# Random-feature attention ahead of a gated MLP: q, k and v loaded in runs of 512 bytes

## The chip, the core and the metric

The kernel runs on one core of a Trainium2 chip. A core has five instruction engines, each of which works through its own queue in order and waits on semaphores for the others: TensorE (PE; matmuls and transposes, with the loading of weights listed apart as PEld), VectorE (DVE), ScalarE (ACT), GpSimd (POOL) and SyncE (SP), which here issues all DMAs. Matmuls write to PSUM, all other data lies in SBUF, and 16 DMA engines move data between SBUF and device memory. The metric is the device time of one execution in microseconds; before and after are compared by the median of several runs. A profiled execution gives the trace: start, length and releaser of every instruction, and the clock that TensorE was granted.

## What is computed

The reference, cut to its core (m is 128 random features, D is 64, eight batches, eight heads, 576 positions):

```python
scale = 1.0 / np.sqrt(np.sqrt(D))
def phi(x):
    proj = np.einsum('bhsd,md->bhsm', x, omega)
    h = proj - np.sum(x * x, axis=-1, keepdims=True) / 2.0
    h = h - np.max(h, axis=-1, keepdims=True)
    return np.exp(h) / np.sqrt(m)
q_p, k_p = phi(q * scale), phi(k * scale)
kv = np.einsum('bhsm,bhsd->bhmd', k_p, v)
z = np.sum(k_p, axis=2)
num = np.einsum('bhsm,bhmd->bhsd', q_p, kv)
den = np.einsum('bhsm,bhm->bhs', q_p, z)[..., None] + 1e-06
x = num / den    # then 4608 rows of 512, heads side by side
g = x @ w_gate
out = (g * (1.0 / (1.0 + np.exp(-g))) * (x @ w_val)) @ w_out
```

The weights are stored as 64-bit floats (512 x 1536, 512 x 1536 and 1536 x 512); q, k, v and omega as 32-bit.

## The kernel before

**Attention.** Work goes in groups of G = 256 positions of a pair of heads (512 values of 64: four blocks of 128 rows, CH = 2 chunks for each of two heads). 576 is 2 x 256 + 64, so a batch has eight such groups and one group of rests (`gr is None`) with the last 64 positions of all eight heads. A step takes two groups at once: in the first six steps two of k, then one of q and one of k, at the end two of q. There are 72 steps. Step n goes through these functions, some of them a step or more late (KLAG, NLAG and the like):

- `load` (into `nat`) and `load_v` (into `v0` to `v7`, or `vrest`), both by `load_group`. Position r + 2p + c stands on partition p as chunk c: two neighbouring positions of a head are 512 contiguous bytes in memory. Before, the tile's layout is (chunk, head, 64), so that each of them is a run of 256 bytes of its own.
- `st_transpose`: four transposes (L370) turn a `nat` into `pt`, ACT copies it to `x` (L378), POOL squares `nat` into `sq` (L377).
- `st_project`: 16 matmuls with omega into `pp` (L393), one for each group, chunk and half of the 128 partitions. A half of the partitions is one of the two heads.
- `st_max`: DVE sums the squares (L404), takes the maxima (two of L411 a step) and makes the bias `st` (L413, L414). `st_exp`: ACT takes eight exponentials (L425) into the features `ph`.
- `k_accumulate`: matmuls of `ph` with a block of `v` (L528) into the PSUM tile `kvacc`, which holds four heads. A block of v has 65 columns, the last being ones, so that column 64 collects z. When all of a batch's positions are in, `kv_finalize` lets ACT copy the tile to `kvr` (L441), 16 times in all. In batches 4 to 7 PE then transposes z out of it (`zp`, L447), and z goes by way of device memory to a tile `zt` on all partitions.
- q's side: `q_transpose` (`ptq`, L552, copied to `qt`). In batches 0 to 3 `q_mult` multiplies by the 65 columns of `kvr` and divides by the last one; in batches 4 to 7 `q_den` multiplies `ph` by `zt` on POOL (`jk`, L488), DVE sums it, and `q_norm` scales `ph`. `q_out` writes the result as `x` of the MLP, split in two parts `xh` and `xl` whose sum it is.

**Weights.** They come as pairs of 32-bit words. `convert_all` loads each of 36 pieces raw (tile `st0` to `st11`, a name shared with the statistics; L225 for w_gate), makes 32-bit floats of it in one step on ACT (`wc`, L260), five on DVE (L262 to L270) and one on POOL (L272), and stores it. Later the pieces are read back and split into `whi` and `wlo` (L242, L243).

**MLP.** `stream` goes over tiles of 256 or 512 rows and sets of three 128-column blocks of the hidden width: three products for each of gate (`g`, L641) and value (`v`, L641; the same letter as the attention's v in a trace's rows), then `hh` and `hl` (L724, L725), then the product with w_out (`o`, L650).

**Order.** A table of steps says how much of the MLP and how many ticks of the conversion stand between the parts of a step (`CLOSE` for the first steps, `GROUPED` after). The order in which the rows of the program reach each engine's queue is not this one alone: the tile framework moves instructions by a cost model of its own, in which the length of a load counts. So an edit to a load can move instructions of other engines.

Of the kernel before, what the change touches and what calls it, by code (L numbers as in the profile page):

```python
# [23 lines left out]
def kernel(  # L24
# [76 lines left out]

    NR = S // G
    kgroups = [(pr, t * G) for pr in range(NPAIR) for t in range(NR)]
    kgroups.insert(len(kgroups) // 2, None)
# [18 lines left out]

    def pairs_of(gr):
        return [(2 * c, 2 * c + 1) for c in range(CH)] if gr is None else [gr[:1]] * CH

# [177 lines left out]

    vtile = [att.tile([P, CH, 2, VW], F32, name=f"v{i}", bufs=1) for i in range(NVF)]
    vrest = [att.tile([P, 2 * CH, 2, VW], F32, name=f"vrest{i}", bufs=1) for i in range(1)]
    for t in vtile:
        nc.gpsimd.memset(t[:, :, :, D:VW], 1.0)
    for t in vrest:
        nc.gpsimd.memset(t, 0.0)
        for c in range(CH):
# [7 lines left out]
    def load_group(t, src, b, gr, v_):  # L325
        if gr is not None:
            pr, r = gr
            nc.sync.dma_start(
                t[:, :, :, 0:D],
                src[b, 2 * pr : 2 * pr + 2, r : r + G, :].rearrange("h (p c) d -> p c h d", c=CH),  # L330
            )
            return
        for c in range(CH):
            for j, pr in enumerate(pairs_of(gr)[c]):
                nc.sync.dma_start(
                    t[j * RES : (j + 1) * RES, 2 * c + j if v_ else c, :, 0:D],
                    src[b, 2 * pr : 2 * pr + 2, S - RES : S, :].rearrange("h p d -> p h d"),
                )
# [98 lines left out]

    def kv_finalize(b, a2):
        acc = kvacc.pop((b, a2))
        raw = att.tile([P, 4, VW], F32, name=f"kvr{b}_{a2}", tag="kvr", bufs=4)  # L440
        nc.scalar.copy(raw, acc)  # L441
        for j in range(2):
            kvst[b, 2 * a2 + j] = raw[:, 2 * j : 2 * j + 2, :]
        if b >= BPOOL:

            zp = ps_att(f"zp{b}_{a2}", [4, P])
            nc.tensor.transpose(zp, raw[:, :, D], ident)  # L447
            zs = att.tile([4, P], F32, name=f"zs{b}_{a2}", tag="zs")
            nc.scalar.copy(zs, zp)
            zd = dram.tile([4, P], F32, name=f"zd{b}_{a2}", tag="zd", bufs=4)  # L450
            nc.sync.dma_start(zd, zs)
            zds[b, a2] = zd
# [18 lines left out]
    def q_den(n):  # L471

        n -= JLAG
        for _, b, g, gr in slots(n, "q"):
            if b < BPOOL:
                continue
            ph = box["q", b, g].rearrange("p c (h m) -> p c h m", m=M)
            jk = att.tile([P, CH, 2, M], F32, name=f"jk{b}_{g}", tag="jx")
            if gr is None:
                for c in range(CH):  # L480
                    for j, pr in enumerate(pairs_of(gr)[c]):
                        rows = slice(j * RES, (j + 1) * RES)
                        zt = zbc[b, pr // 2][rows, 2 * (pr % 2) : 2 * (pr % 2) + 2, :]
                        nc.gpsimd.tensor_tensor(jk[rows, c], ph[rows, c], zt, op=ALU.mult)
            else:
                pr = gr[0]
                zt = zbc[b, pr // 2][:, 2 * (pr % 2) : 2 * (pr % 2) + 2, :]
                nc.gpsimd.tensor_tensor(  # L488
                    jk, ph, zt.rearrange("p (o h) m -> p o h m", o=1).broadcast_to([P, CH, 2, M]), op=ALU.mult
                )  # L490
            dn = att.tile([P, 3, CH, 2], F32, name=f"dj{b}_{g}", tag="dj", bufs=6)
            nc.vector.tensor_reduce(dn[:, 0], jk, axis=AX.X, op=ALU.add)
            nc.vector.tensor_scalar_add(dn[:, 1], dn[:, 0], EPS)
            nc.vector.reciprocal(dn[:, 2], dn[:, 1])
            dns[b, g] = dn
# [14 lines left out]
    def k_accumulate(n, half):  # L510
# [3 lines left out]
        for b, g, gr, c in ks[half * len(ks) // 2 : (half + 1) * len(ks) // 2]:  # L514
# [4 lines left out]
            for j, pr in enumerate(pairs_of(gr)[c]):  # L519
                a2 = pr // 2  # L520
                first = (b, a2) not in kvacc
                if first:
                    kvacc[b, a2] = ps_k.tile([P, 4, VW], F32, name=f"kvacc{b}_{a2}", tag="kv")
                acc = kvacc[b, a2]
                done.setdefault((b, a2), []).append(pr)
                last = LAST[pr] == (g, c)
                for hh in range(2):
                    nc.tensor.matmul(  # L528
                        acc[:, 2 * (pr % 2) + hh, :],
                        ph[:, c, hh * M : (hh + 1) * M],  # L530
                        vt[:, 2 * c + j if gr is None else c, hh, :],
                        start=first and hh == 0,
                        stop=last,
                        skip_group_check=True,
                    )
# [6 lines left out]

    def q_transpose(n):
        m = n
        todo = [(b, g) for _, b, g, gr in slots(n - TLAG, "q") if b < BPOOL]
        todo += [(b, g) for _, b, g, gr in slots(n - NLAG, "q") if b >= BPOOL]
        for b, g in todo:
            ph = box.pop(("q", b, g))
            pt = (ps_moe if m < EARLY else ps_att)(f"ptq{b}_{g}", [P, 2, G])
            for hh in range(2):  # L550
                for c in range(CH):
                    nc.tensor.transpose(pt[:, hh, c * P : (c + 1) * P], ph[:, c, hh * M : (hh + 1) * M], ident)  # L552
            qts[b, g] = att.tile([P, 2, G], F32, name=f"qt{b}_{g}", tag="qt")
            nc.scalar.copy(qts[b, g], pt)

# [291 lines left out]
```

## Time and profile before

| | us |
|---|---|
| three runs | 1250.28, 1251.25, 1261.83 |
| median | 1251.25 |
| profiled execution | 1254.07 |
| its span, first to last instruction | 1252.3 |
| DVE, ACT, POOL: share of the span busy | 42%, 48%, 40% |
| DMA: packets; of them under 512 B | 157,692; 119,680 |
| DMA: moved, mean rate | 97.80 MB, 78 GB/s |

The page gives busy time for each engine, then slices of the span in tenths, and the chain of work that ended last. Rows of groups name line, engine, operation, output <- input and count. In rows of waits the first name waits for the second, then total time, times and the longest. Rows of the timeline give start, length, engine and line, with the idle time ahead in brackets. "SPq" is SP's issuing of a DMA. TensorE's granted clock is 1.00 at full speed and 0.50 at half.

### The profile page before, as it was taken

What the parts mean: (1) busy time and instruction counts of PE and PEld (TensorE: products, weight loads), DVE (VectorE), ACT (ScalarE), POOL (GpSimd) and SP (SyncE); (2) the same over time, 40 slices, a digit from 0 to 9 for tenths busy, and PEclk for the clock granted to TensorE, in tenths of its full rate; (3) what the DMA queues carried; (4) which work ended last, traced back from release to release, by engine and by line L of the source; (5) the groups of instructions that cost most, each with busy time, mean ns of one, the idle gap of its engine ahead of it and who ended that gap; (6) DMA issues with size and microseconds to landing.
All of it is one profiled execution on the core that took longest, in us unless ns stands there. A gap on an engine that the chain in (4) does not pass through costs nothing.

```text
span 1252.3 us, 19047 instructions
## 1 busy us (share of the span) xinstructions
PE 1217.5 (97%) x7137; PEld 1013.1 (81%) x7137; DVE 530.8 (42%) x1080; ACT 599.4 (48%) x1344; POOL 506.3 (40%) x448
## 2 busy tenths in 40 slices
PE   6999999999999999999999998999999999999998
PEld 5988877888778888778788876888787778888887
DVE  4887696556752344334434342233433311111112
ACT  3787755554354554556555443564644323221211
POOL 3333443645362213445544432554654314242421
PEclk7999999999999999999999998999999999999999
DMA  6555555343442222222222321221211111010112
GB/s 162 146 122 157 149 135 176 105 141 115 127 126 64 53 71 64 66 66 63 73 52 60 82 52 31 69 59 52 58 43 34 36 24 51 26 51 26 51 31 54
DMA packets 157692, 97.80 MB, mean 78 GB/s; under 512 B 119680, under 2 KB 132000, under 8 KB 157600
## 3 DMA queue, kind: packets, MB, share of 16 engines
q1 hardware_dynamic: 157600, 96.59, 29.0%
q8 instruction: 56, 0.92, 0.3%
q14 instruction: 36, 0.29, 0.1%
HBM read 77.66 MB, written 18.89 MB: 77 GB/s over the span
## 4 chain that ended last, share of the span: by engine, by line
PE 68%; DVE 2%; POOL 1%; ACT 1%; issue 0%; DMA 0%; SPq 0%; POOLq 0%; DVEq 0%
PE o L650 19%; PE g L641 19%; PE v L641 19%; PE pp L393 3%; PE kvacc L528 2%; PE ptq L552 2%; PE xt L607 2%; PE pt L370 1%; PE po L569 1%; POOL hl L725 1%; DVE st L266 0%; DMA nat<-in_k_dram 0%; DVE sl L721 0%; ACT ph L425 0%; DVE st L411 0%
## 5 line engine op out<-in xcount | busy, mean ns | idle before, releaser
L725 POOL TENSOR_TENSOR hl<-sl,hh 128x512 fp32r<-128x512 f32 (+1 forms) x120 | 142.3, 1190 | 208.0 <-ACT hh L724 207.9
L641 PE MATMUL g<-xh,whi 128*128 128x512 f32 (+1 forms) x480 | 181.6, 379 | 1.7 <-DVE sl L721 1.7
L641 PE MATMUL v<-xh,whi 128*128 128x512 f32 (+1 forms) x480 | 180.1, 375 | 2.7 <-DVE acc L674 2.7
L641 PE MATMUL g<-xh,wlo 128*128 128x512 f32 (+1 forms) x480 | 178.1, 372 | 0.0
L641 PE MATMUL g<-xl,whi 128*128 128x512 f32 (+1 forms) x480 | 178.1, 371 | 0.0
L243 POOL TENSOR_TENSOR wlo<-wraw,whi 128x512 fp32r<-128x512 f32 x108 | 139.0, 1299 | 95.6 <-ACT whi L242 94.1
L641 PE MATMUL v<-xh,wlo 128*128 128x512 f32 (+1 forms) x480 | 177.4, 370 | 0.0
L641 PE MATMUL v<-xl,whi 128*128 128x512 f32 (+1 forms) x480 | 177.3, 369 | 0.0
L650 PE MATMUL o<-whi,hh 128*128 128x512 f32 x432 | 173.4, 401 | 2.8 <-ACT hh L724 2.8
L425 ACT ACTIVATE ph<-pp,st 128x128 f32<-128x128 f32 x576 | 157.9, 384 | 32.8 <-DVE st L414 32.5
L650 PE MATMUL o<-whi,hl 128*128 128x512 f32 x432 | 170.6, 395 | 2.4 <-POOL hl L725 2.4
L650 PE MATMUL o<-wlo,hh 128*128 128x512 f32 x432 | 169.8, 393 | 0.0
L724 ACT CAST hh<-sl 128x512 fp32r<-128x512 f32 (+1 forms) x120 | 69.5, 581 | 207.5 <-DVE sl L721 207.1
L721 DVE TENSOR_TENSOR sl<-v,sl 128x512 f32<-128x512 f32 (+1 forms) x120 | 75.7, 633 | 181.3 <-PE v L641 179.3
L674 DVE TENSOR_TENSOR acc<-o,acc 128x512 f32<-128x512 f32 x108 | 74.1, 689 | 185.1 <-PE o L650 185.0
L377 POOL TENSOR_TENSOR sq<-nat 128x512 f32<-128x512 f32 x72 | 77.8, 1081 | 179.2 <-DMA nat<-in_k_dram 132.0
L411 DVE TENSOR_REDUCE st<-pp 128x4 f32<-128x512 f32 x144 | 93.7, 683 | 51.2 <-PE pp L393 51.0
L242 ACT CAST whi<-wraw 128x512 fp32r<-128x512 f32 x108 | 66.4, 623 | 100.0 <-PE v L641 61.2
L641 PEld LDWEIGHTS v<-xh,whi 128*128 128x128 f32 x480 | 90.6, 189 | 20.1 <-DVE acc L674 3.1
L641 PEld LDWEIGHTS g<-xh,whi 128*128 128x128 f32 x480 | 90.9, 190 | 19.7 <-issue 2.7
L641 PEld LDWEIGHTS g<-xh,wlo 128*128 128x128 f32 x480 | 91.0, 190 | 16.0 <-issue 0.4
L641 PEld LDWEIGHTS v<-xh,wlo 128*128 128x128 f32 x480 | 90.5, 189 | 15.2
(67 smaller groups left out, 1886.0 us busy)
## 6 DMA issues: line engine op xcount, KB each, us to landing
wraw<-wscr SPq DMA_DIRECT2D x108, 256.0 KB, 2.7
wscr<-wc SPq DMA_DIRECT2D x36, 256.0 KB, 2.3
out_dram<-acc SPq DMA_DIRECT2D x72, 128.0 KB, 2.3
nat<-in_k_dram SPq DMA_DIRECT2D x64, 128.0 KB, 3.0
v<-in_v_dram SPq DMA_DIRECT2D x64, 128.0 KB, 3.0
nat<-in_q_dram SPq DMA_DIRECT2D x64, 128.0 KB, 2.7
st<-in_moe_w_gate_dram SPq DMA_DIRECT2D x12, 512.0 KB, 5.2
st<-in_moe_w_val_dram SPq DMA_DIRECT2D x12, 512.0 KB, 4.2
```

What stands on the lines that cost most here:

```text
L242: nc.scalar.copy(hi, raw)
L243: nc.gpsimd.tensor_tensor(lo, raw, hi.bitcast(F32), op=ALU.subtract)
L377: nc.gpsimd.tensor_tensor(sq, nat, nat, op=ALU.mult)
L393: nc.tensor.matmul(pp[hh][:, i, c, :], x[r, i, c * P : (c + 1) * P], omT[r], start=True, stop=True)
L411: nc.vector.tensor_reduce(st[:, 1, :, :, hh], pp[hh], axis=AX.X, op=ALU.max, negate=True)
L425: nc.scalar.activation(ph[:, c, hh * M : (hh + 1) * M], pp[hh][:, i, c, :], AF.Exp, bias=st[:, 3, i, c, hh : hh + 1], scale=1.0,)
L641: nc.tensor.matmul(ps, a_[:, ws], b_[:, c, :], start=n == 0, stop=n == 3 * NC - 1)
L650: nc.tensor.matmul(ps, a_[:, ts_], b_, start=first and n == 0, stop=last and n == 2)
L674: nc.vector.tensor_tensor(a_, po, a_, op=ALU.add)
L721: nc.vector.tensor_tensor(h, pv, h, op=ALU.mult)
L724: nc.scalar.copy(hh, h)
L725: nc.gpsimd.tensor_tensor(hl, h, hh.bitcast(F32), op=ALU.subtract)
```

## The change

Chunks lie inside heads. The layout of a loaded group becomes (head, chunk, 64), so that two neighbouring positions of a head land as one run of 512 bytes. The transposes (L370) take the same addresses as before, but what comes out has the two positions on the two halves of the partitions and the two heads as blocks, so a projection's half is now a chunk. A small function `place` tells the readers of `ph` where chunk c of head hh stands.

v's tile becomes (head, 130): one column of ones, two chunks of 64, one column of ones. The block of chunk 0 is columns 0 to 64 with the ones ahead, that of chunk 1 is columns 65 to 129 with the ones behind. So the accumulator gets 66 columns: chunk 0 writes columns 0 to 64, chunk 1 columns 1 to 65, and z arrives in two parts. `kv_finalize` copies 4 x 66 columns and adds column 0 to column 65 on POOL. The group of rests stays as it was.

```diff
+    def place(gr, c, hh):
+        return (c, hh) if gr is None else (hh, c)
...
-    vtile = [att.tile([P, CH, 2, VW], F32, name=f"v{i}", bufs=1) for i in range(NVF)]
+    vtile = [att.tile([P, 2, 1 + CH * D + 1], F32, name=f"v{i}", bufs=1) for i in range(NVF)]
...
-        nc.gpsimd.memset(t[:, :, :, D:VW], 1.0)
+        for o in (0, 1 + CH * D):
+            nc.gpsimd.memset(t[:, :, o : o + 1], 1.0)
...
-                t[:, :, :, 0:D],
-                src[b, 2 * pr : 2 * pr + 2, r : r + G, :].rearrange("h (p c) d -> p c h d", c=CH),
+                t[:, :, 1 : 1 + CH * D] if v_ else t.rearrange("p h c d -> p h (c d)"),
+                src[b, 2 * pr : 2 * pr + 2, r : r + G, :].rearrange("h (p c) d -> p h (c d)", c=CH),
...
-        raw = att.tile([P, 4, VW], F32, name=f"kvr{b}_{a2}", tag="kvr", bufs=4)
-        nc.scalar.copy(raw, acc)
+        both = att.tile([P, 4, 1 + VW], F32, name=f"kvr{b}_{a2}", tag="kvr", bufs=4)
+        nc.scalar.copy(both, acc)
+        raw = both[:, :, 1:]
+        nc.gpsimd.tensor_tensor(raw[:, :, D], raw[:, :, D], both[:, :, 0], op=ALU.add)
...
-                    jk, ph, zt.rearrange("p (o h) m -> p o h m", o=1).broadcast_to([P, CH, 2, M]), op=ALU.mult
+                    jk, ph, zt.rearrange("p h (o m) -> p h o m", o=1).broadcast_to([P, 2, CH, M]), op=ALU.mult
...
-                    kvacc[b, a2] = ps_k.tile([P, 4, VW], F32, name=f"kvacc{b}_{a2}", tag="kv")
+                    kvacc[b, a2] = ps_k.tile([P, 4, 1 + VW], F32, name=f"kvacc{b}_{a2}", tag="kv")
...
+                    e, o = place(gr, c, hh)
+
+                    z = 0 if gr is not None and c == 0 else 1
                     nc.tensor.matmul(
-                        acc[:, 2 * (pr % 2) + hh, :],
-                        ph[:, c, hh * M : (hh + 1) * M],
-                        vt[:, 2 * c + j if gr is None else c, hh, :],
+                        acc[:, 2 * (pr % 2) + hh, z : z + VW],
+                        ph[:, e, o * M : (o + 1) * M],
+                        vt[:, 2 * c + j, hh, :] if gr is None else vt[:, hh, c * VW : (c + 1) * VW],
...
-                    nc.tensor.transpose(pt[:, hh, c * P : (c + 1) * P], ph[:, c, hh * M : (hh + 1) * M], ident)
+                    e, o = place(gr, c, hh)
+                    nc.tensor.transpose(pt[:, hh, c * P : (c + 1) * P], ph[:, e, o * M : (o + 1) * M], ident)
```

The order of instructions moves in the first part of the program. The lines of the changed program are numbered 6 to 14 higher there: L404, L411, L413 and L414 are L412, L419, L421 and L422, and L260 to L272 are L266 to L278.

DVE's queue near its start, before. `st_0` and `st_1` are statistics of steps 0 and 1, `pp0` and `pp1` the two halves of a projection, `wc0_0` the first weight piece in conversion and `st0_0` its raw words:

```order
L404 TENSOR_REDUCE st_2_221<-sq_2_222 128x8
L411 TENSOR_REDUCE st_0_142<-pp0_0_151 128x4
L411 TENSOR_REDUCE st_0_142<-pp1_0_152 128x4
L404 TENSOR_REDUCE st_3_263<-sq_3_264 128x8
L413 SCALAR_TENSOR_TENSOR st_0_142<-st_0_142 128x8
L411 TENSOR_REDUCE st_1_176<-pp0_1_203 128x4
L414 SCALAR_TENSOR_TENSOR st_0_142<-st_0_142 128x8
L411 TENSOR_REDUCE st_1_176<-pp1_1_204 128x4
L413 SCALAR_TENSOR_TENSOR st_1_176<-st_1_176 128x8
L262 TENSOR_SCALAR wc0_0_167<-wc0_0_167 128x512
L414 SCALAR_TENSOR_TENSOR st_1_176<-st_1_176 128x8
```

The same place on DVE in the changed program:

```order
L412 TENSOR_REDUCE st_2_229<-sq_2_230 128x8
L268 TENSOR_SCALAR wc0_0_175<-wc0_0_175 128x512
L270 TENSOR_SCALAR wc0_0_175<-wc0_0_175 128x512
L272 SCALAR_TENSOR_TENSOR st0_0_169<-st0_0_169,wc0_0_175 128x512
L419 TENSOR_REDUCE st_0_150<-pp0_0_159 128x4
L419 TENSOR_REDUCE st_0_150<-pp1_0_160 128x4
L419 TENSOR_REDUCE st_1_184<-pp0_1_211 128x4
L421 SCALAR_TENSOR_TENSOR st_0_150<-st_0_150 128x8
L419 TENSOR_REDUCE st_1_184<-pp1_1_212 128x4
L422 SCALAR_TENSOR_TENSOR st_0_150<-st_0_150 128x8
```

Three steps of the weight's conversion have moved ahead of the maxima of steps 0 and 1.

ACT at the same place, before:

```order
L378 COPY x_1_175<-pt_1_170 128x512
L378 COPY x_2_220<-pt_2_215 128x512
L260 ACTIVATE wc0_0_167<-st0_0_161 128x512
L425 ACTIVATE ph0_0_185<-pp0_0_151,st_0_142 128x128 x2
L425 ACTIVATE ph0_0_185<-pp1_0_152,st_0_142 128x128 x2
```

And in the changed program:

```order
L386 COPY x_1_183<-pt_1_178 128x512
L266 ACTIVATE wc0_0_175<-st0_0_169 128x512
L266 ACTIVATE wc1_0_322<-st1_0_171 128x512
L386 COPY x_2_228<-pt_2_223 128x512
L386 COPY x_3_270<-pt_3_265 128x512
L433 ACTIVATE ph0_0_193<-pp0_0_159,st_0_150 128x128 x2
```

A second weight piece and the copy of step 3's transposes now stand ahead of the first exponentials. On SP the two raw pieces moved likewise, from behind step 3's loads of k to ahead of them.

PE where z of batch 4's second half is transposed, before (in brackets what a row waits for):

```order
L528 MATMUL kvacc4_1_4429<-v7_101,ph1_38_4695 128x65 x4
L641 MATMUL v11_11_4965<-xh2_1314,whi11_1_4178 128x512
L641 MATMUL v11_11_4965<-xl2_1315,whi11_1_4178 128x512
L641 MATMUL v11_11_4965<-xh2_1314,wlo11_1_4179 128x512
L447 MATMUL zp4_1_4939<-ident_87,kvr4_1_4937 4x128 [waits Activation_49]
```

And in the changed program:

```order
L541 MATMUL kvacc4_1_4446<-v7_101,ph1_38_4712 128x65 x4
L655 MATMUL v11_11_4983<-xh2_1326,whi11_1_4194 128x512
L655 MATMUL v11_11_4983<-xl2_1327,whi11_1_4194 128x512
L655 MATMUL v11_11_4983<-xh2_1326,wlo11_1_4195 128x512
L457 MATMUL zp4_1_4957<-ident_87,kvr4_1_4954 4x128 [waits Pool_49]
```

The place is the same, but the transpose waits for POOL, which has the add in its queue between two subtractions `hl`.

More of the change, by code (lines that the diff above doesn't have):

```diff
@@ L544, in q_transpose @@
         m = n
-        todo = [(b, g) for _, b, g, gr in slots(n - TLAG, "q") if b < BPOOL]
-        todo += [(b, g) for _, b, g, gr in slots(n - NLAG, "q") if b >= BPOOL]
-        for b, g in todo:
+        todo = [(b, g, gr) for _, b, g, gr in slots(n - TLAG, "q") if b < BPOOL]
+        todo += [(b, g, gr) for _, b, g, gr in slots(n - NLAG, "q") if b >= BPOOL]
+        for b, g, gr in todo:
             ph = box.pop(("q", b, g))
```

## The prediction

> **What bounds the kernel now.** First the page: busy time, the slices and the chain.
>
> ```profile
> span 1252.3 us, 19047 instructions
> ...
> PE 1217.5 (97%) x7137; PEld 1013.1 (81%) x7137; DVE 530.8 (42%) x1080; ACT 599.4 (48%) x1344; POOL 506.3 (40%) x448
> ...
> PE   6999999999999999999999998999999999999998
> ...
> PEclk7999999999999999999999998999999999999999
> ...
> PE 68%; DVE 2%; POOL 1%; ACT 1%; issue 0%; DMA 0%; SPq 0%; POOLq 0%; DVEq 0%
> ```
>
> TensorE (PE) is busy 1217.5 of 1252.3 us, and the chain that ended last runs over it; DMA has 0% of the chain. A change of loads can only win the 34.8 us in which PE is idle, and what is lost while its clock is low. So next I ask where PE idles and for whom: PE's own waits, then its busy time by stretch (columns: length, then busy time of PE, PEld, DVE, ACT and POOL, granted clock, DMA share, GB/s).
>
> ```profile
> PE pt_om L306 <- DMA om<-in_omega_dram: 5.2, 1, 5.2
> PE kvacc L528 <- ACT ph L425: 5.0, 1, 5.0
> PE pt L370 <- DMA nat<-in_k_dram: 1.0, 2, 0.5
> ...
> 0.00:40.00 40.00, 28.73 (x195) 25.90 (x196) 21.49 (x41) 17.60 (x52) 15.30 (x31) 0.79 0.60 148
> 40.00:170.00 130.00, 124.52 (x1052) 111.35 (x1052) 100.97 (x247) 99.86 (x277) 50.80 (x44) 0.99 0.55 142
> ...
> 16.00:18.00 2.00, 0.00 (x0) 0.00 (x0) 1.21 (x4) 0.00 (x0) 0.00 (x0) 0.52 1.11 341
> 32.00:34.00 2.00, 2.00 (x15) 1.93 (x15) 1.97 (x7) 1.14 (x2) 0.00 (x0) 0.71 0.25 57
> ```
>
> In the whole run PE waits 1.0 us for a load of k, and 5.2 us at the very start for omega. A third of its idle time, 11.3 us, lies in the first 40 us, and 5.5 us in the next 130. The clock falls to half near 16 us and comes back near 33, so some 14 us of busy time there (from 19.3 on, below) take about 7 us more than at full clock. That start is where this change can be felt.
>
> **The start, step by step.** The timeline there (start, length, what; in brackets the idle time ahead and who ended it):
>
> ```profile
> 10.20 1.29 SPq L328 DMA_DIRECT2D nat<-in_k_dram  x2
> 12.23 1.19 SPq L225 DMA_DIRECT2D st<-in_moe_w_gate_dram  x2
> 13.19 1.28 DVE L411 TENSOR_REDUCE st<-pp 128x4 f32<-128x512 f32 x2
> 16.36 0.68 DVE L411 TENSOR_REDUCE st<-pp 128x4 f32<-128x512 f32 x1
> 18.32 0.66 ACT L260 ACTIVATE wc<-st 128x512 f32<-128x512 f32 x1 [4.83 <-DMA st<-in_moe_w_gate_dram]
> 18.88 4.22 ACT L425 ACTIVATE ph<-pp,st 128x128 f32<-128x128 f32 x16
> 19.01 0.43 DVE L262 TENSOR_SCALAR wc<-wc 128x512 f32<-128x512 f32 x1 [1.77 <-ACT wc L260]
> 19.29 2.48 PE L528 MATMUL kvacc<-v,ph 128*128 128x65 f32 x10 [5.03 <-ACT ph L425]
> 19.93 0.69 DVE L266 SCALAR_TENSOR_TENSOR st<-st,wc 128x512 int32<-128x512 int32 x1
> 30.86 1.29 DVE L411 TENSOR_REDUCE st<-pp 128x4 f32<-128x512 f32 x2 [3.14 <-PE pp L393]
> 31.97 0.59 ACT L378 COPY x<-pt 128x512 f32<-128x512 f32 x1 [2.78 <-PE pt L370]
> 34.31 2.18 ACT L425 ACTIVATE ph<-pp,st 128x128 f32<-128x128 f32 x8
> ```
>
> The first exponentials (18.88) stand on ACT behind the first weight conversion, which waits 4.83 us for a raw w_gate piece issued at 12.23. PE has nothing else and idles 5.03 us: so the clock falls. The wait is for a weight and not for q, k or v.
>
> **The change, part by part.**
>
> Loads. The 192 large loads of q, k and v keep their 128 KB but go in 512 B runs. Bounds for a 512 B packet are a 256 B and a 1 KB one:
>
> ```profile
> nat<-in_k_dram SPq DMA_DIRECT2D x64, 128.0 KB, 3.0
> DMA packets 763, 0.18 MB, mean 92 GB/s; under 512 B 763, under 2 KB 763, under 8 KB 763
> q1 hardware_dynamic: 763, 0.18, 40.8%
> ...
> DMA packets 351, 0.35 MB, mean 350 GB/s; under 512 B 9, under 2 KB 351, under 8 KB 351
> q1 hardware_dynamic: 351, 0.35, 101.2%
> ...
> POOL sq L377 <- DMA nat<-in_k_dram: 132.0, 38, 18.1
> SPq L328 <- PE pt L370: 68.6, 21, 19.1
> ```
>
> Between 9 and 11 us 763 packets, nearly all of 256 B, took 0.408 x 2 us x 16 engines = 13.1 us, 17 ns each. Between 15 and 16 us 351, nearly all of 1 KB, took 16.2 us, 46 ns each. On a line through both a 512 B packet takes 27 ns (an estimate). A load is then 256 x 27 / 16 = 0.43 us of packets against 512 x 17 / 16 = 0.54: 0.11 us less, while its landing takes 3.0 us. In steady state that is worth nothing: POOL's 132 us of waiting for k end at a DMA, but the load was issued late, because its buffer was still in use (SP waits 68.6 us for the transposes out of it alone). Ahead of the w_gate pieces stand nine or so loads, so the weight lands 0 to 1.0 us sooner. I take 0 for the sum, as SP issues such loads 0.6 us and more apart (the rows at 10.20 and 12.23 hold two each), further than their packets take.
>
> The Trainium skill ("DMA: Bandwidth & Descriptors", Specifications) puts the line rate at 512 B or more and says that shorter transfers do read-modify-write. Here a quarter of the bytes took 17 ns against 46, not as long or longer, so the trace shows no such penalty on these reads. If 512 B runs still halved the loads' time, as the page's sentence suggests, the w_gate pieces would come at most some 2.4 us sooner, and the sum would gain that.
>
> Order. The front of the program is in another order; TensorE's last change of place lies about 1,000 of its 5,987 rows in, within the first 170 us. SP now issues the w_gate pieces ahead of step 3's k, whose two issues are the 1.29 us at 10.20: at about 10.9 instead of 12.23. With the same 6.1 us to ACT's start they are there at 17.0. On DVE three conversion steps on that piece now stand ahead of the four maxima (L411) of steps 0 and 1, which before began at 13.19. So: 17.0 + 0.66 (ACT) + 0.43 + 0.43 + 0.69 = 19.2, then four maxima of 0.68 and two small steps of 0.16: 22.2. The first exponentials come at about 22.3 instead of 18.88, 3.4 us late (2.4 with the faster loads). In that time PE does step 3's transposes and a few projections, some 1.4 us of work that it did later before, so its gap grows by about 2 us.
>
> That is given back. Before, DVE then idled 3.14 us (30.86) and ACT 2.78 us (31.97), because steps 2 and 3 had not been projected. Now their copies stand ahead of the exponentials. From 22.2 DVE has 20 operations to the last input of step 3's exponentials: six sums and conversions of 0.69, four of 0.43, four maxima of 0.68 and six small ones of 0.16, 9.5 us: 31.7 without any wait, some 33 with a wait or two for POOL. Before, these exponentials began at 34.31. So the start lies between 2.5 us sooner and 3.4 us later; I take 0, as the chain that is late at 22 is level by 34. The low clock adds about 3.5 us to either side (half of a 7 us longer or shorter spell). Between 40 and 170 us PE's idle 5.5 us will fall in other places; bounds 5.5 us either way, taken 0.
>
> The sum of the two columns of ones. Each of the 16 finished halves of a head group gets an add on POOL (128x4). For the eight of batches 4 to 7 PE transposes the result (zp) three matmuls behind the last accumulation:
>
> ```profile
> 392.91 0.74 POOL L725 TENSOR_TENSOR hl<-sl,hh 128x256 fp32r<-128x256 f32 x1 [0.70 <-ACT hh L724]
> 411.78 1.04 POOL L377 TENSOR_TENSOR sq<-nat 128x512 f32<-128x512 f32 x1 [18.14 <-DMA nat<-in_k_dram]
> ...
> 399.89 0.38 ACT L441 COPY kvr<-kvacc 128x260 f32<-128x260 f32 x1 [0.26 <-PE kvacc L528]
> 400.43 0.27 PE L447 MATMUL zp<-ident,kvr 128*4 128x128 f32 x1
> ...
> 453.53 1.28 POOL L725 TENSOR_TENSOR hl<-sl,hh 128x512 fp32r<-128x512 f32 x1
> 454.47 0.38 ACT L441 COPY kvr<-kvacc 128x260 f32<-128x260 f32 x1 [0.20 <-PE kvacc L528]
> ```
>
> POOL's subtraction takes 0.74 us for 256 elements and 1.28 for 512, so a very short operation takes about 0.2 (the line's end at 0). The hand-over from ACT to PE took 400.43 - 400.27 = 0.16; a second one with the add between costs 0.36, and PE has no cover, since zp is next in its queue. Eight such places give 2.9 us. At 400 us POOL had been idle since 393.65, and at 454 it finished at 454.81, as ACT's copy ended. Behind the add stand hl and jk, which need ACT anyway. Bounds: 0, and one whole 1.28 us operation ahead in each of eight: 13 us. I take 2.9, since POOL was free at both places shown. For batches 0 to 3 the users of the sum come steps later: 0. Eight more memsets and four more columns in a copy lie under waits: 0 (POOL's first square waits for k).
>
> Unaltered: the number and shape of matmuls, reductions and exponentials.
>
> Sum: loads 0, start 0, 40 to 170 us 0, adds 2.9. The profiled execution took 1254.07 us, which gives 1257.0; it was 2.8 over the median of the three runs, and on that median the time is 1251.25 + 2.9 = 1254.2.
>
> **The rivals.**
>
> Faster: the clock returns sooner. After the gap the projections of two steps now stand between the accumulations, so PE's work is denser than from 19 to 33 us. If the clock then comes back 7 us earlier that is 3.5 us, and with the start 2.5 us sooner and the loads' 1.0: 1254.2 - 7 = 1247. Against it: the gap ahead is longer.
>
> The Trainium skill ("TensorE: Matmul & The Clock Gate", Part 1) has the low clock follow an idle window of about 3.4 us, and end after about 3.4 us of sustained work. The fall fits the 5.03 us gap here; the return does not, 33 us being 14 us behind the restart. By the page's rule both programs would pay 3.4 us and this rival would gain nothing by density.
>
> Slower: the add becomes a wait of PE for POOL's queue. If at the eight places POOL sits in an operation or in a wait for ACT, each costs up to 1.9 us (1.28 + 0.36 and a wait), 15 us: 1266. It decides from 1.6 us a place, which makes 12.5. Against it POOL's idle rows above and its 40%.
>
> Start late and not given back: 3.4 us for the exponentials and 3.5 for the clock, with the 2.9: 1261. For it: SP's later loads wait for the step 3 transposes, which are now late.
>
> **How the numbers follow.** Forecast (1249 to 1258) 0.60; start late 0.17; clock sooner 0.15; POOL's queue 0.08. The range 1243 to 1263 leaves out POOL's queue and about as much in the tails. About 1% (12.5 us) is what a measurement can tell here, the three runs of before being 11.6 us apart. Below 1238.7 lies only a sum of all gains, 0.03; above 1263.8 POOL's queue and a little of the late start, 0.09; the rest, 0.88, is within.
>
> **What would show it.** Packets under 512 B fall by 98,304 (192 x 512) and landing of k stays within 0.3 us of 3.0. PE's longest early wait is for ph again, ending near 22.5. DVE's first L411 follows the wc steps. PE's waits gain zp from POOL, about 0.35 each. PE's busy time beyond 400 us stays within 1%. Wrong would be: PE's gap under 4 us or a clock that stays full (then faster), zp waits over 1 us, or matmuls into the accumulators dearer than before.

## The result and the profile after

The changed kernel takes 1264.14 us (median of 13 runs, 1257.43 to 1269.91), the kernel before 1251.25 (13 runs, 1248.38 to 1261.83): ratio 1.010, 95% interval 1.0083 to 1.0117. It is slower by 12.9 us, and 1.1 us outside the range of the prediction. Its profiled execution took 1261.46 us, 7.4 us more than that of the kernel before (1254.07), so the profiles below show a little over half of what separates the medians.

The page of the changed kernel, busy time and DMA:

```profile
span 1259.7 us, 19078 instructions
...
PE 1224.2 (97%) x7137; PEld 1016.2 (81%) x7137; DVE 526.7 (42%) x1080; ACT 597.9 (47%) x1342; POOL 509.4 (40%) x472
...
PEclk7799999999999999999999999999999999999999
...
DMA packets 108540, 97.80 MB, mean 78 GB/s; under 512 B 21376, under 2 KB 82848, under 8 KB 108448
...
nat<-in_k_dram SPq DMA_DIRECT2D x64, 128.0 KB, 2.6
```

The loads do what was meant: 98,304 packets fewer under 512 B, and a load of k lands in 2.6 us instead of 3.0. Yet TensorE (PE) is busy 6.7 us longer with the same 7137 instructions. Work that is the same and takes longer points at the clock, and the second slice of the PEclk row has gone from 9 to 7. Busy time by stretch of the changed kernel (columns as in the prediction):

```profile
0.00:40.00 40.00, 27.40 (x147) 23.04 (x149) 16.70 (x34) 16.03 (x46) 15.25 (x40) 0.69 0.55 150
40.00:80.00 40.00, 35.24 (x291) 32.74 (x289) 31.81 (x67) 25.27 (x78) 17.03 (x17) 0.84 0.54 155
80.00:125.00 45.00, 42.04 (x393) 36.89 (x392) 37.45 (x97) 36.35 (x111) 20.26 (x19) 1.00 0.48 138
400.00:1000.00 600.00, 595.91 (x3407) 480.96 (x3406) 223.92 (x471) 311.71 (x667) 265.32 (x238) 1.00 0.21 58
```

The same of the kernel before, for the second and third stretch and the long one:

```profile
40.00:80.00 40.00, 37.60 (x355) 34.33 (x354) 33.33 (x77) 32.05 (x100) 17.43 (x15) 0.96 0.54 136
80.00:125.00 45.00, 43.17 (x399) 39.31 (x398) 35.07 (x98) 36.84 (x109) 14.85 (x13) 1.00 0.60 156
400.00:1000.00 600.00, 594.49 (x3360) 479.46 (x3359) 222.60 (x469) 310.70 (x666) 259.03 (x224) 0.99 0.23 57
```

In the first 40 us PE ends 147 instructions instead of 195, in the next 40 us 291 instead of 355; from 80 us on the two are nearly level. So the loss that these profiles show is made in the first 80 us. What that delays is the MLP: its first product, the start at the left of the range in these two rows, comes 14.1 us later. Before:

```profile
L641 PE MATMUL g<-xh,whi x19: 280/284/477, 111.1 to 137.6; 128*128 128x256 f32 x12, 128*128 128x512 f32 x7
```

Changed:

```profile
L655 PE MATMUL g<-xh,whi x12: 280/282/365, 125.2 to 132.7; 128*128 128x256 f32 x12
```

PE alone in stretches cut at its spells of half clock (length, PE's busy time, granted clock, DMA share, GB/s), in the changed kernel:

```profile
15.00:43.00 28.00, 24.49 (x123) 0.51 0.46 128
43.00:56.00 13.00, 10.22 (x96) 1.00 0.53 151
56.00:63.00 7.00, 6.82 (x39) 0.51 0.69 203
63.00:73.00 10.00, 8.20 (x81) 1.00 0.52 141
73.00:77.00 4.00, 4.00 (x23) 0.57 0.63 195
```

And in the kernel before:

```profile
16.00:34.00 18.00, 14.71 (x82) 0.53 0.65 168
34.00:74.00 40.00, 37.60 (x374) 1.00 0.56 136
74.00:78.00 4.00, 4.00 (x26) 0.57 0.36 108
```

These rows show the spells: 27.3 us from 15 on, 6.8 from 56 and 3.4 from 73, against 17.1 and 3.4 us before (lengths from windows of 1 us, each counted as twice what is missing to full clock). Over the whole profile, which runs 2 us past the last instruction, the clock is at half for 45.0 us, against 33.3. Half of that difference, 5.9 of the 7.4 us, is what the low clock takes. (The record of the clock begins at 8.4 us here and at 12.7 before; the start is left out of it, see the last section.)

The start of the changed kernel, with what PE and ACT wait for:

```profile
9.17 1.02 SPq L231 DMA_DIRECT2D st<-in_moe_w_gate_dram  x2
10.33 2.29 SPq L336 DMA_DIRECT2D nat<-in_k_dram  x4
13.88 0.66 ACT L266 ACTIVATE wc<-st 128x512 f32<-128x512 f32 x1 [6.74 <-DMA st<-in_moe_w_gate_dram]
15.96 1.09 PE L378 MATMUL pt<-ident,nat 128*128 128x128 f32 x4 [5.58 <-DMA nat<-in_k_dram]
19.25 4.23 ACT L433 ACTIVATE ph<-pp,st 128x128 f32<-128x128 f32 x16 [1.52 <-DVE st L422]
19.67 1.11 PE L541 MATMUL kvacc<-v,ph 128*128 128x65 f32 x4 [1.08 <-ACT ph L433]
30.25 0.58 ACT L386 COPY x<-pt 128x512 f32<-128x512 f32 x1 [6.26 <-PE pt L378]
34.41 0.58 ACT L386 COPY x<-pt 128x512 f32<-128x512 f32 x1 [3.58 <-PE pt L378]
```

PE now waits 5.58 us for step 3's k, whose loads stand behind the two of w_gate on SP. SP issues them hardly later than before (from 10.33 on, against 10.20), but the transposes of them begin at 15.96 and not at 13.30. What has changed ahead of them is the two pieces of w_gate, 512 KB each: from 12 to 14 us the DMA engines move 368 GB/s, where the mean is 78. That the k waits behind these bytes is my reading; no run takes it alone. ACT waits 9.8 us in two pieces for the transposes of steps 4 and 5, because the copies of these stand ahead of step 2's exponentials, which come at 34.89 us.

### The profile page after: what moved, and what is told of

Read it like the earlier page. It is cut to its first block, busy times and chain, and to the rows that moved or that the text cites. A ratio compares the mean times of both kernels' runs of the same rounds, so it can differ in the third digit from the quotient of the medians.

```text
span 1259.7 us, 19078 instructions
## 1 busy us (share of the span) xinstructions
PE 1224.2 (97%) x7137; PEld 1016.2 (81%) x7137; DVE 526.7 (42%) x1080; ACT 597.9 (47%) x1342; POOL 509.4 (40%) x472
## 4 chain that ended last, share of the span: by engine, by line
PE 67%; DVE 2%; POOL 1%; ACT 1%; issue 0%; DMA 0%; SPq 0%; POOLq 0%; DVEq 0%
PE o L664 19%; PE g L655 19%; PE v L655 19%; PE pp L401 3%; PE kvacc L541 2%; PE ptq L566 2%; PE xt L621 2%; PE pt L378 1%; PE po L583 1%; POOL hl L739 1%; DVE st L272 0%; DVE sl L735 0%; ACT ph L433 0%; DMA nat<-in_k_dram 0%; DVE st L419 0%
## 5 line engine op out<-in xcount | busy, mean ns | idle before, releaser
L419 DVE TENSOR_REDUCE st<-pp 128x4 f32<-128x512 f32 x144 | 93.3, 684 | 51.2 <-PE pp L401 51.0
L401 PE MATMUL pp<-omT,x 64*128 64x128 f32 x1152 | 105.0, 300 | 4.6 <-ACT x L386 3.4
L401 PEld LDWEIGHTS pp<-omT,x 64*128 64x128 f32 x1152 | 86.5, 198 | 27.0 <-issue 12.6
```

The lines of the kernel that those rows point to most:

```text
L401: nc.tensor.matmul(pp[hh][:, i, c, :], x[r, i, c * P : (c + 1) * P], omT[r], start=True, stop=True)
L419: nc.vector.tensor_reduce(st[:, 1, :, :, hh], pp[hh], axis=AX.X, op=ALU.max, negate=True)
```

## The experiments

Two theories stood at first. A: the order costs the time; the scheduler moved the first third of the queues because the loads have another price in its model. B: the layout costs it (adds on POOL, 66 columns, two columns of ones). To hold an order, a table of names for each engine is chained by edges that fix the order of issue and add no wait; an instruction that only the changed kernel has stands right behind the one that it follows there.

```diff
+    table = json.loads(zlib.decompress(base64.b64decode(ORDER)))
+    traced = {i.name: i for i in nc.cur_bb.bb.instructions}
...
+        for before, name in zip(row, row[1:]):
+            tc.add_manual_dep(
+                traced[name], before,
+                mybir.DependencyInfo(mybir.DependencyClass.NoSync, mybir.DependencyReason.DATA),
```

All results (time: median; clock: median granted clock of the runs timed; product: mean of span times granted clock over these runs; first g and half clock: of the profiled execution, in us, the latter with the 2 us past the last instruction). The row of the kernel before is over 78 runs beside the others; old_code_new_order has 6 runs, hold_gate, new_order_filled, qk_only and v_only have 4 each, the rest 10 to 13.

| kernel | time | ratio to before, 95% interval | clock | product | first g | half clock |
|---|---|---|---|---|---|---|
| before | 1251.6 | | 0.989 | 1235.3 | 111.1 | 33.3 |
| changed | 1264.14 | 1.010 (1.0083 to 1.0117) | 0.978 | 1235.1 | 125.2 | 45.0 |
| new_code_old_order | 1250.72 | 0.9997 (0.9983 to 1.0012) | 0.988 | 1233.8 | 107.0 | 34.2 |
| old_code_new_order | 1270.81 | 1.0136 (1.0106 to 1.0166) | 0.978 | 1240.4 | 128.3 | 57.1 |
| first38 | 1253.09 | 1.0008 (0.9985 to 1.0031) | 0.987 | 1234.2 | 114.8 | 33.3 |
| first22 | 1253.55 | 1.0019 (1.0001 to 1.0037) | 0.986 | 1234.3 | 114.6 | 27.9 |
| hold_gate | 1266.44 | 1.0111 (1.0059 to 1.0163) | 0.980 | 1238.7 | 132.0 | 72.6 |
| new_order_filled | 1265.42 | 1.0105 (1.0086 to 1.0123) | 0.980 | 1238.2 | 123.9 | 57.9 |
| old_order_filled | 1252.10 | 1.0007 (0.9982 to 1.0031) | 0.990 | 1237.4 | 109.4 | 27.0 |
| new_order_filled2 | 1253.01 | 1.0016 (0.9994 to 1.0039) | 0.991 | 1241.5 | 114.5 | 26.7 |
| old_order_filled2 | 1247.17 | 0.9971 (0.9959 to 0.9983) | 0.996 | 1239.9 | 102.4 | 16.9 |
| before_filled2 | 1248.78 | 0.9966 (0.9951 to 0.9982) | 0.995 | 1240.9 | 105.9 | 13.6 |
| qk_only | 1261.25 | 1.0107 (1.0066 to 1.0147) | 0.982 | 1236.0 | 120.1 | 38.0 |
| v_only | 1259.96 | 1.0065 (1.0045 to 1.0085) | 0.982 | 1237.4 | 112.3 | 34.2 |

### The order and the code, crossed

> The changed kernel, with every engine's instructions held in the order that they have in the kernel before (the ones that the change adds stand right behind the instruction that they follow in the changed kernel). Theory A, the order costs the 12 us: the time comes back to that of before, ratio 0.997 to 1.003, the first product of the MLP starts at 110 to 113 us, half clock lasts 30 to 36 us in all. Theory B, the layout itself costs it (the adds on POOL, the accumulator of 66 columns, the columns of ones ahead and behind): ratio 1.008 to 1.012 and a first product near 125 us as in the changed kernel. Theory C, both share it: ratio 1.004 to 1.007.

> The kernel before, with every engine's instructions held in the order that they have in the changed kernel. Theory A: ratio 1.008 to 1.013, a first product of the MLP at 123 to 128 us, half clock of 42 to 48 us. Theory B: ratio 0.997 to 1.003, first product at 110 to 113 us. Theory C: 1.004 to 1.007. If the order counts on the loads that land 0.4 to 0.5 us sooner in the changed kernel, this one is the slowest of all, 1.012 to 1.018.

The changed code in the old order takes 0.9997 of the time before, and the old code in the new order 1.0136. Theory A holds, B falls: adds, 66 columns and columns of ones cost nothing that these runs can tell. In the new order the old code is the slowest, as the expectation had it for loads that land later: 1.0136 against 1.010, the intervals just overlapping. Its first product, at 128.3 us, and its half clock, 57.1 us, lie over what A expected (123 to 128 and 42 to 48); in new_code_old_order the first product, at 107.0, came before the 110 to 113. The first two stretches of new_code_old_order:

```profile
0.00:40.00 40.00, 30.80 (x225) 27.72 (x225) 23.41 (x42) 20.64 (x63) 16.75 (x41) 0.79 0.57 158
40.00:80.00 40.00, 37.77 (x351) 34.77 (x352) 35.27 (x85) 31.84 (x97) 17.71 (x18) 0.96 0.50 143
```

And of old_code_new_order:

```profile
0.00:40.00 40.00, 25.73 (x132) 21.70 (x132) 16.51 (x34) 13.68 (x39) 14.10 (x30) 0.68 0.59 145
40.00:80.00 40.00, 36.38 (x271) 33.58 (x270) 26.71 (x58) 25.39 (x77) 15.36 (x13) 0.76 0.58 145
```

PE's count and the clock go with the order and not with the code: 225 and 351 at 0.79 and 0.96, near the 195 and 355 of the kernel before, with the same clock; 132 and 271 at 0.68 and 0.76, near the 147 and 291 of the changed kernel at 0.69 and 0.84.

### How much of the order

first38 holds the old order only to the end of step 3's exponentials, first22 only to the end of step 0's, and then queues everything else behind; the rest is the scheduler's.

```diff
+        for i in traced.values():
+            if i.engine == traced[row[-1]].engine and i.name not in row and int(i.name[2:]) > 91:
+                tc.add_manual_dep(i, row[-1], ...)
```

> The changed kernel, with every engine's instructions held in the order of the kernel before only up to the last exponential of step 3, which ends at 38 us there; behind it the scheduler orders them as it likes, and again takes the weights' conversions earlier than the kernel before does (the first of w_val behind x_9 instead of behind x_10). Theory A1, the first 40 us decide (the loads of w_gate ahead of step 3's k, the copies x_4 and x_5 ahead of step 2's exponentials): ratio 0.997 to 1.003 and half clock of 30 to 37 us. Theory A2, the conversions that run ahead between 40 and 110 us decide: ratio 1.006 to 1.012. Both halves: 1.003 to 1.006.

> The changed kernel, held in the order of the kernel before only up to the last exponential of step 0, which is over near 21 us: 39 instructions of TensorE, 16 of VectorE, 13 of ScalarE, 24 loads. The scheduler orders the rest, with the weights' conversions ahead as in the 38 us variant. If the first 22 us decide: ratio 0.998 to 1.004. If the places from 22 to 38 us (x_4 and x_5 ahead of step 2's exponentials) matter by themselves and come back: ratio 1.006 to 1.012.

Both come back to the time of before, though from there on the scheduler again runs the weights' conversions ahead of the old order. So the conversions that run ahead between 40 and 110 us do not cost the time there (theory A2 falls), and it is enough to hold the first 39 instructions of PE, 16 of DVE, 13 of ACT and 24 loads. Which of these places it takes, the two runs do not say. first22 is at most 0.4% slower than before.

hold_gate asks whether the one moved pair of loads is the root.

```diff
+        if n == LA:
+            third.append([i for i in nc.cur_bb.bb.instructions if i.engine == mybir.EngineType.SP][-1])
...
+                if n < 2:
+                    tc.add_manual_dep(got.ins, third[0].name, ...)
```

> The changed kernel with one constraint on the order: the first two loads of w_gate are issued behind step 3's loads of k. The scheduler orders all the rest. If the 5.6 us that TensorE waits for step 3's k is the root of the loss: pt_3 starts near 12 us instead of 16, half clock falls from 45 to 30 to 38 us, ratio 0.997 to 1.004. If it is only one of many moves: ratio 1.005 to 1.011, with half clock above 40 us.

It isn't mended by that: 1.0111, with half clock from 14 to 62 us in the profiled execution, the slowest of its four. But the scheduler made a third order around the edge: it put four loads of vrest ahead of step 3's k, which SP issued at 11.93 (10.20 before), so pt_3 began at 14.56 and not near 12, and PE then waited 4.09 us for a copy. So this run does not say what the pair alone costs. PE in hold_gate:

```profile
14.56 1.09 PE L387 MATMUL pt<-ident,nat 128*128 128x128 f32 x4 [3.36 <-DMA nat<-in_k_dram]
19.73 0.80 PE L410 MATMUL pp<-omT,x 64*128 64x128 f32 x4 [4.09 <-ACT x L395]
```

### The clock or the waits

The table's product says more than the ratios. Span times granted clock is 1235.3 us before and 1235.1 after (standard deviations of 2.3 and 1.6 us), and stays between 1233.8 and 1241.5 for all fourteen kernels, while their times go from 1247 to 1271. Counted in full-speed time the kernels take nearly the same, and most of what separates their times is the clock; not all, as old_code_new_order has 5.1 of its 19.2 us in the product. The product counts idle time at half clock by half too, so it can't tell by itself what brought the clock down. This leads to theory D (the order costs time by the half clock that its waits bring on) and its rival E (the order's waits cost it whatever the clock). A fill tells them apart: transposes of the identity into a PSUM tile that real work overwrites later, put on PE where it waited, with all other places held by the tables.

```diff
+                    if (b, a2) == (0, 0):
+                        spare = kvacc[b, a2].rearrange("p a d -> p (a d)")[:, 0:P]
+                        for _ in range(25):
+                            nc.tensor.transpose(spare, ident, ident)
```

> The changed kernel in its own order, with 25 transposes of the identity matrix into the still unused accumulator put on TensorE between pt_2 and pt_3, where it waited 5.6 us: nothing else moves. Theory D, the loss is TensorE's half clock, which that gap brings on: the clock stays full through 15 to 34 us, half clock falls from 45 us to below 25 us, and 5 to 10 us of the 12.6 come back, ratio 1.000 to 1.006. Theory E, the loss is the waits of the order themselves (PE for ACT's copies behind exponentials), whatever the clock: TensorE waits longer instead, ratio 1.008 to 1.012.

> The changed kernel in the order of the kernel before, with 20 transposes of the identity matrix between pt_3 and the first product of k and v, where TensorE waited 4.1 us. Theory D: half clock falls from 33 us to about 12 to 20 us, and 3 to 7 us are won, ratio 0.994 to 0.998. Theory E: the first 40 us are bound by ScalarE's and VectorE's steps, and nothing is won, ratio 0.998 to 1.002.

Neither gave D's gain; both ratios (1.0105 and 1.0007) lie where E had them. But the first fill was short. 25 transposes took 2.89 us and left 2.15 and 1.34 us open, and the clock fell at 17 us. PE in new_order_filled:

```profile
11.01 2.89 PE L608 MATMUL kvacc<-ident 128*128 128x128 f32 x25
16.05 0.82 PE L449 MATMUL pt<-ident,nat 128*128 128x128 f32 x4 [2.15 <-DMA nat<-in_k_dram]
19.75 1.11 PE L616 MATMUL kvacc<-v,ph 128*128 128x65 f32 x4 [1.34 <-ACT ph L504]
```

In old_order_filled the clock stayed full up to 94 us and then fell for 13.7 us at a wait of 1.57 us, which gave the lead back in that execution. PE by stretch:

```profile
10.00:94.00 84.00, 75.97 (x738) 1.00 0.59 164
94.00:109.00 15.00, 13.91 (x71) 0.54 0.26 71
```

And the end of that wait on the timeline:

```profile
95.09 0.66 PE L688 MATMUL xt<-ident,xn 128*128 128x128 f32 x2 [1.57 <-DVE xn L667]
```

So both were tried again with every gap filled that these traces showed.

```diff
+    def fill(spare, n):
+        for _ in range(n):
+            nc.tensor.transpose(spare, ident, ident)
...
+                        fill(kvacc[b, a2].rearrange("p a d -> p (a d)")[:, 0:P], FILL["kv"])
...
+        fill(pp[0][:, 0, 0, :], FILL["pp"].get(n, 0))
...
+            fill(pt[:, 0, 0:P], FILL["ptq"].get((b, g), 0))
...
+            fill(po[:, 0:P], FILL["xt"].get((b, g), 0))
```

> The changed kernel in its own order, with 86 transposes of the identity matrix in the five places of the first 60 us where TensorE waited: 44 behind pt_2, 6 behind pt_3, 12 ahead of the first product of k and v, 7 behind pt_5, 17 ahead of ptq0_0 (0.115 us each at full clock). The first fill left 2.2 us of the first gap and all the others open, and the clock fell at 17 us instead of 15. Theory D, the time is set by how long the clock is at half: it stays full to 60 us, half clock falls from 45 to 10 to 25 us, span times clock stays at 1235 to 1240, ratio 0.994 to 1.002. Theory E, the order is bound by the chain through ScalarE and VectorE even at full clock: TensorE then runs ahead, waits elsewhere and the clock falls all the same, ratio 1.004 to 1.012.

> The changed kernel in the order of the kernel before, with 36 transposes of the identity matrix behind pt_3 (20 before) and 16 ahead of xt1_0, where the profiled run of the first fill waited 1.6 us and lost the clock from 94 to 109 us. Theory D: half clock near 13 us (the spells at 343 and 763 us and the end stay), a granted clock of 0.993 to 0.997 in most runs, ratio 0.991 to 0.996. If the spell at 94 us only moves elsewhere: ratio 0.998 to 1.002 as with the first fill.

Theory D holds: E's range, 1.004 to 1.012, lies above the whole interval. In its own, slow order the changed kernel is back at 1253.01 us, 1.0016 of before, with nothing moved and 86 transposes added. From 10 to 40 us the clock is full. One spell of 10.2 us remained, behind a wait of 0.99 us at 40, and half clock came to 26.7 us, a little over what D expected, as is the product: 1241.5, 6.4 us more full-speed time than the changed kernel without the fill. PE in new_order_filled2, by stretch and at that wait:

```profile
10.00:40.00 30.00, 28.91 (x259) 1.00 0.69 193
40.00:51.00 11.00, 10.59 (x56) 0.53 0.72 208
51.00:125.00 74.00, 69.99 (x655) 1.00 0.52 149
...
40.41 0.69 PE L479 MATMUL pp<-omT,x 64*128 64x128 f32 x4 [0.99 <-ACT x L463]
```

The old order with both gaps filled beats both kernels, 0.9971, its clock full from 9.9 us, where its record begins, to 350 us in the profiled execution:

```profile
0.00:100.00 100.00, 90.91 (x864) 1.00 0.54 154
100.00:350.00 250.00, 242.08 (x1480) 1.00 0.46 140
```

Its ratio came out at 0.997, above the 0.991 to 0.996 expected: its product, 1239.9, is 4.6 us over that of before, so of the 8.7 us that 0.007 more clock is worth about half was paid back in time at full clock; I take that for the fill itself and for waits that the faster work ran into.

### Does the layout have a part in the gain, or one half of the change in the loss?

> The kernel before, with its loads of 256 B and its layout, held in its own order, with the same 52 transposes of the identity matrix (36 behind pt_3, 16 ahead of xt1_0). If the gain of the second fill (ratio 0.9971) is the clock's alone: ratio 0.996 to 0.999, a granted clock of 0.993 to 0.997, span times clock at 1240 us. If the layout has a part in it (its loads land sooner, so that TensorE waits less behind the fill): ratio 0.999 to 1.003.

0.9966 with the old loads and layout, against 0.9971: the gain needs the fill alone, and runs of 512 B add nothing to it that these runs can tell.

qk_only takes the change of q and k alone, v_only that of v alone; each got its order from the scheduler.

```diff
+            if v_:
+                nc.sync.dma_start(
+                    t[:, :, :, 0:D],
+                    src[b, 2 * pr : 2 * pr + 2, r : r + G, :].rearrange("h (p c) d -> p c h d", c=CH),
+                )
+                return
...
-        nc.gpsimd.tensor_tensor(raw[:, :, D], raw[:, :, D], both[:, :, 0], op=ALU.add)
```

That is qk_only; v_only has the same with `not v_`, keeps the add, and puts q's and k's blocks back:

```diff
-        return (c, hh) if gr is None else (hh, c)
+        return c, hh
```

> Only q and k in runs of 512 B (chunks inside heads, projections by halves); v, its accumulator of 65 columns and its single column of ones as before, no adds on POOL. The scheduler orders it: the loads of step 3's k stand behind one load of w_gate instead of behind two (changed kernel) or none (before), two conversions stand ahead of x_2 on ScalarE as in the changed kernel, and TensorE takes step 2's products ahead of step 3's as before. The theory of the order and the clock: time is 1233 to 1237 us over the granted clock, whatever the clock; with step 2's products in front I expect 0.984 to 0.989, ratio 1.000 to 1.005. The theory that q's and k's part of the change costs the time: 1.008 to 1.012.

> Only v in runs of 512 B, with its columns of ones ahead and behind, the accumulator of 66 columns and the adds on POOL; q and k in runs of 256 B as before. The scheduler orders it: one load of w_gate and one conversion ahead, TensorE as in the kernel before up to the first products of step 3. The theory of the order and the clock: time is 1234 to 1238 us over the granted clock, clock 0.984 to 0.989, ratio 1.000 to 1.005. The theory that v's part (adds, 66 columns) costs the time: 1.008 to 1.012.

The ratios, 1.0107 and 1.0065, miss what I expected of the order; each is from four runs. By its ratio alone qk_only lies where the rival had it (1.008 to 1.012). Against that rival stand new_code_old_order, which has both halves at 0.9997, and the halves' sum, which is more than the whole (1.010). Their products, 1236.0 and 1237.4, lie at that of before or within 2.1 us of it, and their clock is 0.982: once more two orders with two patterns of half clock. What I read from an order, that step 2's products in front would keep the clock, was not enough to foretell it.

## Why the prediction was wrong

The step that failed is "that is given back", with the 0 for the start and the 0 for 40 to 170 us that came of it. It asked when the exponentials are late, and took the clock as an addition of at most 3.5 us. What the runs show in its place: the new order keeps TensorE at half clock longer. By the medians the granted clock is lower by 0.011, which is 13.8 us, and that is the loss.

- **First exponentials.** Foretold for 22.3 us, 3.4 late; they came at 19.25 against 18.88. SP issued the w_gate pieces at 9.17 and not at 10.9, and the first landed 4.7 us later (13.88) and not 6.1, so the conversion was over before the maxima needed DVE.
- **The longest early wait.** Foretold was one for ph, ending near 22.5. It was for step 3's k, 5.58 us ending at 15.96, and the wait for ph was 1.08. The prediction moved w_gate ahead of that k on SP, and gave the k's delay no price.
- **Level by 34 us.** Foretold were step 3's exponentials at 31.7 to 33 us. In the changed kernel steps 2 and 3 go out together from 34.89 on, so step 3 begins near 37.0 (half of 4.24 us later) against 34.31, and step 2, at 27.02 before, is 7.9 us late. Step 4 comes at 45.21 against 38.45: the lag, 7.9, 2.7 and 6.8 us, is not given back. I had counted DVE's operations up to step 3 and left out that PE, at half clock, does the transposes and projections in front of them and that ACT waits for those (6.26 and 3.58 us). In new_order_filled2, the same order with the clock full there, steps 2 and 3 go out at 28.18. ACT's timeline in the changed kernel:

```profile
34.89 4.24 ACT L433 ACTIVATE ph<-pp,st 128x128 f32<-128x128 f32 x16
44.73 0.59 ACT L386 COPY x<-pt 128x512 f32<-128x512 f32 x1 [4.25 <-PE pt L378]
45.21 1.15 ACT L433 ACTIVATE ph<-pp,st 128x128 f32<-128x128 f32 x4
```

In new_order_filled2:

```profile
28.18 4.24 ACT L511 ACTIVATE ph<-pp,st 128x128 f32<-128x128 f32 x16
```

And in the kernel before:

```profile
27.02 2.17 ACT L425 ACTIVATE ph<-pp,st 128x128 f32<-128x128 f32 x8 [1.90 <-DVE st L414]
38.45 1.91 ACT L425 ACTIVATE ph<-pp,st 128x128 f32<-128x128 f32 x7 [1.46 <-DVE st L414]
```

- **The clock.** The low clock lasted 27.3 us and not 17.1, and behind two more waits (1.86 us of PE for ph at 55.66, 1.29 for xn at 72.93) it came back for 6.8 and 3.4 us, where the kernel before had one of 3.4. By the medians of the runs: 0.011 less granted clock on 1250 us is 13.8 us, the whole loss. The rival "the clock returns sooner" had the right quantity and the wrong sign; "start late and not given back" had the sign, at 1261, but for a lateness of the first exponentials that did not come.
- **Loads, 0.** Right: with the order held the change is worth 0.9997. A landing fell by 0.4 us, a little more than the 0.3 allowed. The Trainium skill ("DMA: Bandwidth & Descriptors", Specifications) says that transfers below 512 B do read-modify-write. It gives no rate for them, and the halving that the prediction read into it didn't show: 2.6 us instead of 3.0.
- **Adds, 2.9 us.** The size was about right, the worth not. An add takes 0.20 us (median), and PE's weight loads for zp wait 3.2 us for it in seven places, where they waited 1.0 us for ACT in four before. With the order held that shows neither in the time (0.9997) nor in the product (1233.8). The add's group in the changed kernel:

```profile
L451 POOL TENSOR_TENSOR kvr<-kvr x16: 200/204/675, 39.5 to 905.5; 128x4 f32<-128x4 f32 x16
```

Its waits (us, times, longest):

```profile
PEld zp L457 <- POOL kvr L451: 3.2, 7, 0.6
```

And those before:

```profile
PEld zp L447 <- ACT kvr L441: 1.0, 4, 0.5
```

- **Beyond 400 us.** Right: 595.91 against 594.49 us of PE in 600.
- **The clock's rule.** By the Trainium skill ("TensorE: Matmul & The Clock Gate", Part 1) a low clock ends after some 3.4 us of sustained work. The prediction had seen that it lasts longer, and in the changed kernel one spell lasted 3.4 us and another 27.3. "The fall fits the 5.03 us gap" was read too kindly: the gap began at 14.26 (19.29 less 5.03), and by the prediction's row for 16 to 18 us the clock was at half from 16.1 on, 1.8 us into the gap. The point missed is that a short wait can cost more than its length: behind 0.99 us in new_order_filled2 the clock was at half for 10.2 us, which is 5.1 us of work, and behind the 1.29 us at 72.93 for 3.4 us, which is 1.7.

What stays open: why these orders keep or lose the clock, wait by wait. hold_gate, qk_only and v_only were each foretold wrongly. Nor was it tried what the scheduler's model holds a load of 512 B to cost; that the moved order comes of it is an inference from the change and the two half changes, each of which moved the order in its own way.

## What to carry to other kernels

When TensorE is busy nearly all the time, multiply span by granted clock before looking for a cause: if the product stands still, the question is which short waits brought the low clock on, and filling them can be worth more than a faster load: here 52 idle transposes won 0.3%, and the loads nothing that could be told. Where a scheduler sets the order, an edit to a transfer is also an edit to the order; hold the order of the one kernel on the code of the other, both ways, before giving a price to either. An order that looks even at one late instruction can still lose by the instruction next to it, so follow the busiest engine's gaps and not only the chain that was late.

## What was unexpected of the hardware

- Every spell of half clock in the fourteen profiled executions that ends inside the span lasts a multiple of 3.41 us: 3.4, 6.8, 10.2, 13.7, 17.1, 23.9, 27.3, 30.7 and 47.8 us. After the long gap of the start it took 14 us of unbroken work to come back (before, 19 to 33 us), at 73 us in the changed kernel a single 3.4 us. The spells of full clock between two changes are multiples too (41.0, 433.5, 252.6 and 477.9 us in the kernel before: 12, 127, 74 and 140 of them), so within one execution all changes sit on one grid of 3.41 us.
- The granted clock does not tell of the start. In the kernel before its record begins at 12.67 us with full clock, yet four transposes take 1.10 us at 11.71, as they do at half clock (1.12 at 30.76) and not as at full clock (0.66 at 38.04).
- A wait of 0.99 us (new_order_filled2 at 40 us) was enough for a fall, while one of 2.46 us behind the fill (old_order_filled, ending at 16.86 us) brought none. How long PE was busy in the step of the grid just ahead doesn't decide it alone: 2.42 of 3.41 us from 37.14 on in new_order_filled2, where the clock fell, and 1.64 us from 12.77 on in old_order_filled, where it didn't. The MLP has such spells too: in old_order_filled 3.4 us at 343 behind a wait of 1.8 us, 6.8 at 763 behind waits of 2.0 and 1.3 us. The wait in old_order_filled without a fall:

```profile
16.86 1.47 PE L615 MATMUL kvacc<-v,ph 128*128 128x65 f32 x10 [2.46 <-ACT ph L503]
```

- SP issues a load of two runs of 512 B a partition faster as well: two in 0.92 us and, above, four in 2.29, against two in 1.29 in the prediction's rows.

```profile
16.79 0.92 SPq L336 DMA_DIRECT2D nat<-in_k_dram  x2
```
